# Six units' query softmax as ten per-row exponentials on ScalarE, and another queue for one of the last stores

## Chip, cores and metric

One core of one Trainium2 chip. The metric is device microseconds (us) of one execution. TensorE multiplies matrices, VectorE and GpSimd do elementwise work, ScalarE evaluates functions such as the exponential, and SyncE issues DMAs; ScalarE can issue DMAs too.

## What is computed

A linear attention feeds two gated MLPs. Cut to what matters:

```python
def _attn_ref(q, k, v):                       # 8 batches, 8 heads, 576 tokens, 64 columns
    q_s = q - np.max(q, axis=-1, keepdims=True)
    q_s = np.exp(q_s)
    q_s = q_s / (np.sum(q_s, axis=-1, keepdims=True) + 1e-09)
    k_s = softmax of k over the tokens        # axis=2, written out in the same way
    kv = np.einsum('bhsd,bhse->bhde', k_s, v)
    return np.einsum('bhsd,bhde->bhse', q_s, kv)

# x: 4608 tokens x 512
xn = x / rms(x) * rms_g
x = (silu(xn @ w_gate) * (xn @ w_val)) @ w_out        # d_ff 1536
h = x @ w_in
return (h * sigmoid(1.702 * h)) @ w_out2              # d_ff 2048
```

The query's softmax runs over 64 columns, so each token and head is a row of its own, with its own maximum and its own sum.

## The kernel before

**Units.** Attention is cut into 32 units: one batch and two heads each. In a unit the 576 tokens lie on 128 partitions, as R = 5 rows of each head on a partition, so a tile of queries is 128 partitions x 2 heads x 5 rows x 64 columns: 640 elements on a partition, in ten rows of 64. `unit_steps` gives nine steps for each unit. The steps that matter here:

- `s0`: VectorE reduces the keys to a maximum per column (line 337).
- `s1`: TensorE transposes that maximum (344), VectorE reduces it over the partitions (348), and VectorE takes the queries' maximum of each row, `qm` (351). Then the queries minus `qm` are written in place (352). `side` is GpSimd for units 0 to 7 and VectorE after them.
- `s2`: TensorE spreads the keys' maximum (356), VectorE subtracts it (357).
- `s3`: ScalarE takes the exponential of the keys, `ke`, and of the queries, `qe`, one instruction of 640 elements each (375). VectorE sums each query row into `qs` (381), adds 1e-9 (382) and takes the reciprocal (383); `side` multiplies `qe` by it (384).
- `s4` multiplies keys and values on TensorE (390) and scales the product on VectorE (398 to 407); the last four steps transpose the queries (420) and multiply them by it (441 to 445).

**Order.** All instructions are issued in the order in which the program is written; each engine works its own list in order, and a semaphore holds an instruction back until its inputs are there. Units 0 to 3 run first, interleaved by a sorted table, with little else beside them. Then the first MLP starts. It runs over nine token tiles `j`, and in each tile over slots of matmuls (556 for the gate, the value and, from the second tile on, the output; 586 for the output in the first tile). Units 4 to 7 lie among the slots of `j` = 0. In the same slots the weights are decoded for the first time: ScalarE (152, 153), VectorE (156, 157) and GpSimd (162) turn a fetched piece `stage` into fp32, and ScalarE and GpSimd split it into a high and a low half (165, 166). A matmul of three passes uses the high half in the first two and the low half in the third. The fetch of the next piece is issued after GpSimd's 162.

**End.** The last step of the second MLP writes its output `y` in four parts (p = 5, 3, 4, 2), each of two halves of 128 tokens: SyncE's queue takes the first half, ScalarE's the second (784). A half that crosses a border between token rows takes two stores.

Of the kernel before, what the change touches and what calls it, by code (L numbers as in the profile page):

```python
# [8 lines left out]
F32 = mybir.dt.float32  # L9
# [3 lines left out]
AF = mybir.ActivationFunctionType  # L13
ALU = mybir.AluOpType
AX = mybir.AxisListType
# [5 lines left out]
def attention_glu_mlp(  # L21
# [26 lines left out]
    nc = tc.nc  # L48
    B, H, S, D = q.shape
# [3 lines left out]
    P = 128  # L53

    R = S // P + 1
    FULL = (R - 1) * P
    REST = S - FULL
    NC = DM // P
# [25 lines left out]
    def f(x):  # L84
        return x.bitcast(F32)
# [4 lines left out]
    ap = tc.alloc_tile_pool(name="ap", bufs=1, side="right")  # L90
# [183 lines left out]
    kt, qt, vt = {}, {}, {}  # L274
# [23 lines left out]
    def load_kq(u):  # L298
        b, c = units[u]
        hs = slice(2 * c, 2 * c + 2)  # L300
        if u < NC:

            kt[u], qt[u] = (
                wp.tile([P, 2, R, D], F32, tag="w", bufs=NW, name=f"{n}_raw") for n in "kq"
            )
            pad(kt[u], qt[u])
        else:
            kt[u], qt[u] = k_sb, q_sb
        spread_tokens(kt[u], k[b, hs])
        spread_tokens(qt[u], q[b, hs])  # L310

    def load_v(u):
        b, c = units[u]
        if 2 <= u < NC:
            vt[u] = wp.tile([P, 2, R, VW], F32, tag="w", bufs=NW, name="v_raw")
            pad_v(vt[u])
        else:
            vt[u] = v_sb[u % 2]
        spread_tokens(vt[u], v[b, 2 * c : 2 * c + 2])

    def bank(tag):
        bufs = {"att": 2, "gv": 2, "acc": 4}[tag]
        return ps.tile([P, 512], F32, tag=tag, bufs=bufs, name=f"ps_{tag}")

    def unit_steps(u, tag="att"):
        b, c = units[u]
        st = {}
        kH, kL = kvH[u % 2], kvL[u % 2]

        side = nc.gpsimd if u < 2 * NC else nc.vector  # L330
        whole = u < NC
        if whole:
            kH = kvF[:, u % 2]

        def s0():
            m1 = ap.tile([P, 2, D], F32, tag="m1", bufs=2, name="m1")
            nc.vector.tensor_reduce(
                out=m1, in_=kt[u].rearrange("p h r d -> p h d r"), op=ALU.max, axis=AX.X
            )
            st["m1"] = m1  # L340

        def s1():
            t = bank(tag)
            nc.tensor.transpose(
                t[:, 0:P], st["m1"].rearrange("p h d -> p (h d)"), ident
            )
            m = ap.tile([P, 1], F32, tag="m", bufs=2, name="m")
            nc.vector.reduce_max(out=m, in_=t[:, 0:P], axis=AX.X)
            st["m"] = m
            qm = ap.tile([P, 2, R, 1], F32, tag="qm", bufs=2, name="qm")  # L350
            nc.vector.tensor_reduce(out=qm, in_=qt[u], op=ALU.max, axis=AX.X)
            side.tensor_tensor(qt[u], qt[u], qm.to_broadcast([P, 2, R, D]), op=ALU.subtract)

        def s2():
            t = bank(tag)
            nc.tensor.transpose(t[:, 0:P], st["m"].to_broadcast([P, P]), ident)
            nc.vector.tensor_tensor(
                kt[u],
                kt[u],
                t[:, 0:P]  # L360
                .rearrange("p (h o d) -> p h o d", h=2, o=1)
                .to_broadcast([P, 2, R, D]),
                op=ALU.subtract,
            )

        def s3():
            for n, src in (("k", kt.pop(u)), ("q", qt.pop(u))):
                st[n] = (wp if u < NC else ap).tile(
                    [P, R, 2, D],
                    F32,  # L370
                    tag="w" if u < NC else f"{n}e",
                    bufs=NW if u < NC else 1,
                    name=f"{n}e",
                )
                nc.scalar.activation(st[n].rearrange("p r h d -> p h r d"), src, AF.Exp)  # L375
            if NC <= u + 1 < len(units):
                load_kq(u + 1)
                load_v(u + 1)
            qe = st["q"]
            qs = ap.tile([P, R, 2, 1], F32, tag="qs", bufs=2, name="qs")  # L380
            nc.vector.tensor_reduce(out=qs, in_=qe, op=ALU.add, axis=AX.X)  # L381
            nc.vector.tensor_scalar_add(qs, qs, EPS_SUM)
            nc.vector.reciprocal(out=qs, in_=qs)
            side.tensor_tensor(qe, qe, qs.to_broadcast([P, R, 2, D]), op=ALU.mult)

        def s4():
            t = bank(tag)
            for r in range(R):
                for h in range(2):
                    nc.tensor.matmul(  # L390
                        t[h * D : (h + 1) * D, 0:VW],
                        st["k"][:, r, h],
                        vt[u][:, h, r, :],
                        start=(r == 0),
                        stop=(r == R - 1),
                    )
            rs = ap.tile([P, 1], F32, tag="rs", bufs=2, name="rs")
            nc.vector.tensor_scalar_add(rs, t[:, D : D + 1], EPS_SUM)
            nc.vector.reciprocal(out=rs, in_=rs)
            for h in range(2):  # L400
                a = slice(h * D, (h + 1) * D)
                nc.vector.tensor_scalar_mul(kH[a, a], t[a, 0:D], rs[a])
            if whole:
                return
            for h in range(2):
                a = slice(h * D, (h + 1) * D)
                nc.vector.scalar_tensor_tensor(
                    out=kL[a, a],
                    in0=t[a, 0:D],
                    scalar=rs[a],  # L410
                    in1=f(kH[a, a]),
                    op0=ALU.mult,
                    op1=ALU.subtract,
                )

        def qT(i):
            t = bank(tag)
            width = 0
            for r in halves_of(b)[i]:
                nc.tensor.transpose(  # L420
                    t[:, width : width + P],
                    st["q"][:, r].rearrange("p h d -> p (h d)"),
                    ident,
                )
                width += size(r)
            if whole:
                qF = ap.tile([P, HALF * P + REST], F32, tag="qH", bufs=2, name="qF")[:, :width]
                nc.scalar.activation(qF, t[:, :width], AF.Copy)
                st["q", i] = qF, None, width
                return  # L430
            hi = ap.tile([P, HALF * P + REST], F32R, tag="qH", bufs=2, name="qH")[:, :width]
            lo = ap.tile([P, HALF * P + REST], F32R, tag="qL", bufs=2, name="qL")[:, :width]
            nc.scalar.activation(hi, t[:, :width], AF.Copy)
            nc.vector.tensor_tensor(lo, t[:, :width], f(hi), op=ALU.subtract)
            st["q", i] = hi, lo, width

        def att(i):
            hi, lo, width = st["q", i]
            t = bank(tag)
            if whole:  # L440
                nc.tensor.matmul(t[:, :width], kH, hi, start=True, stop=True)
            else:
                nc.tensor.matmul(t[:, :width], kH, hi, start=True, stop=False)  # L443
                nc.tensor.matmul(t[:, :width], kH, lo, start=False, stop=False)  # L444
                nc.tensor.matmul(t[:, :width], kL, hi, start=False, stop=True)  # L445
            g0 = b * S + (sum(map(size, halves_of(b)[0])) if i else 0)
            done = 0
            while done < width:
                j, o = divmod(g0 + done, T)
                n = min(width - done, T - o)  # L450
                nc.scalar.activation(xraw(j, c)[:, o : o + n], t[:, done : done + n], AF.Copy)
                done += n

        return [
            s0, s1, s2, s3, s4,
            lambda: qT(0), lambda: qT(1), lambda: att(0), lambda: att(1),
        ]
# [404 lines left out]
    with tc.manual_schedule():  # L862
# [94 lines left out]
        for j in range(NTILE):  # L957
# [18 lines left out]
            for slot in range(SLOTS):  # L976
                n, part = divmod(slot, 3)
# [71 lines left out]
        for i in range(-1, END):  # L1049
            if i >= 0:  # L1050
                for c in range(2):
# [4 lines left out]
                        i, t, lambda i=i, c=c: sums(xraw2[i + 1, c], "B", (nc.vector,) * 4)  # L1056
# [64 lines left out]
        for k in range(NT // T * NSET):  # L1121
# [14 lines left out]
            u = ufac.pop(k)  # L1136
# [8 lines left out]
            for p in (6, 7, 5, 3, 1, 4, 2) if k in IN_PIECES else MADE:  # L1145
# [36 lines left out]
                if end and p in (5, 3, 4, 2):  # L1182
                    h, y = (0, y2) if p in (5, 4) else (1, y1)
                    part = slice(0, Q) if p in (5, 3) else slice(Q, DM)
                    for i, queue in enumerate((nc.sync, nc.scalar)):
                        store_out(first_token(g, i, h)[2], y[:, i, :], queue, part)
            if last and not end:
                for h, y in ((0, y2), (1, y1)):
# [49 lines left out]
```

## Time and profile before

| | |
|---|---|
| median of three runs | 1738.14 us (1737.97 to 1739.06) |
| the profiled execution, timed | 1738.99 us |
| its span in the profile | 1737.2 us |
| TensorE busy | 1711.2 us (99%) |
| VectorE busy | 1164.2 us (67%) |
| ScalarE busy | 778.8 us (45%) |
| GpSimd busy | 377.3 us (22%) |
| TensorE clock granted, mean | 0.999 of full speed |

The span runs from the first to the last recorded instruction or transfer; 1.79 us of the timed execution lie around it. Busy shares are means over stages that have different limits, so the stage around the change is what has to be read.

### The profile page before, as it was taken

The page shows a single profiled execution, that of the slowest core. Times are in us where ns is not written, and L with a number is a line of the kernel's source. Part 1 is how long each engine was busy: PE and PEld are TensorE (multiplying, and loading weights), DVE is VectorE, ACT ScalarE, POOL GpSimd, SP SyncE. Part 2 cuts the span into 40 slices and gives each one's busy share as a digit, 9 for nine tenths or more (in the row PEclk, how much of TensorE's full clock was granted, in tenths as well). Part 3 has the DMA queues.
Part 4 walks back from the last instruction along what each step waited for, and adds up shares of the span by engine and source line. Part 5 has one row for each costly group of instructions (what it writes and reads, how often), then busy time and mean ns, then how long its engine had stood idle before and what let it go on. Part 6 is the DMA issues. An engine that isn't in the chain of part 4 may idle for free.

```text
span 1737.2 us, 26461 instructions
## 1 busy us (share of the span) xinstructions
PE 1711.2 (99%) x10002; PEld 1509.9 (87%) x10002; DVE 1164.2 (67%) x1943; ACT 778.8 (45%) x1299; POOL 377.3 (22%) x352
## 2 busy tenths in 40 slices
PE   6999999999999999999999999999999999999998
PEld 4666888888888888888888899999999999999998
DVE  7998668667676676765234367556556887777786
ACT  5775544535455444534222345445445533333332
POOL 5775222222222212211112523110002500000000
PEclk9999999999999999999999999999999999999999
DMA  6564322313322233110001134554444664444432
GB/s 175 170 191 134 103 84 82 97 56 102 96 82 84 69 102 96 58 48 0 25 1 49 52 119 158 176 169 153 146 146 151 226 196 133 134 126 130 134 122 86
DMA packets 207632, 193.64 MB, mean 111 GB/s; under 512 B 58896, under 2 KB 188944, under 8 KB 207504
## 3 DMA queue, kind: packets, MB, share of 16 engines
q1 hardware_dynamic: 197376, 174.11, 32.6%
q10 hardware_dynamic: 10128, 17.83, 2.8%
q8 instruction: 79, 1.29, 0.3%
q14 instruction: 49, 0.40, 0.1%
HBM read 123.21 MB, written 68.68 MB: 110 GB/s over the span
## 4 chain that ended last, share of the span: by engine, by line
PE 89%; DVE 6%; ACT 2%; DMA 1%; issue 1%; POOL 0%; SPq 0%; DVEq 0%; ACTq 0%; POOLq 0%
PE ps_gv L556 29%; PE ps_out L1150 20%; PE ps_in L738 20%; PE ps_acc L556 14%; DVE xr L533 1%; PE ps_acc L586 1%; PE ps_att L390 1%; DVE sqa L521 1%; PE ps_att L420 1%; DVE w L157 1%; DVE w L156 0%; DMA stage<-in_moe_w_gate_dram 0%; PE ps_att L443 0%; PE ps_att L445 0%; PE ps_att L444 0%
## 5 line engine op out<-in xcount | busy, mean ns | idle before, releaser
L738 PE MATMUL ps_in<-xf,w2i 128*128 128x384 f32 x2016 | 350.3, 335 | 0.0
L738 PEld LDWEIGHTS ps_in<-xf,w2i 128*128 128x128 f32 x2016 | 349.9, 188 | 0.3 <-ACT h L750 0.2
L556 PE MATMUL ps_gv<-xs,wg 128*128 128x512 f32 x1296 | 320.4, 395 | 1.3 <-POOL xs L548 0.7
L556 PE MATMUL ps_gv<-xs,wv 128*128 128x512 f32 x1296 | 317.9, 394 | 1.6 <-POOL wv L166 1.5
L556 PEld LDWEIGHTS ps_gv<-xs,wg 128*128 128x128 f32 x1296 | 240.7, 188 | 58.8 <-DVE xs L548 2.9
L556 PEld LDWEIGHTS ps_gv<-xs,wv 128*128 128x128 f32 x1296 | 239.5, 188 | 52.0 <-POOL wv L166 3.0
L556 PE MATMUL ps_acc<-u,wo 128*128 128x512 f32 x1152 | 283.5, 395 | 0.0
L1150 PE MATMUL ps_out<-w2o,uf 128*128 128x256 f32 x2268 | 271.6, 282 | 0.0
L1150 PEld LDWEIGHTS ps_out<-w2o,uf 128*128 128x128 f32 x2268 | 269.6, 189 | 1.2 <-DVE uf L827 0.2
L556 PEld LDWEIGHTS ps_acc<-u,wo 128*128 128x128 f32 x1152 | 212.1, 188 | 44.2
L981 ACT ACTIVATE s<-ps_gv 128x512 f32<-128x512 f32 x108 | 64.6, 598 | 379.0 <-PE ps_gv L556 378.8
L166 POOL TENSOR_TENSOR wo<-raw,wo 128x512 fp32r<-128x512 f32 x96 | 126.7, 1320 | 490.4 <-ACT wo L165 381.1
L987 DVE TENSOR_TENSOR s<-s,ps_gv 128x512 f32<-128x512 f32 x108 | 73.5, 680 | 177.5 <-PE ps_gv L556 167.3
L723 ACT ACTIVATE h<-h 128x384 f32<-128x384 f32 x144 | 74.2, 525 | 111.6 <-DVE h L762 88.4
L162 POOL TENSOR_TENSOR w<-w,stage 128x512 int32<-128x512 int32 x56 | 76.4, 1364 | 195.6 <-PE ps_gv L556 61.9
L630 DVE TENSOR_TENSOR raw<-raw 128x256 f32<-128x256 f32 (+1 forms) x236 | 106.1, 492 | 9.4 <-DMA raw<-w2d 7.3
L762 DVE TENSOR_TENSOR h<-h,ps_in 128x384 f32<-128x384 f32 x144 | 77.8, 553 | 48.2 <-PE ps_in L738 48.1
L823 ACT ACTIVATE uf<-raw 128x1792 fp32r<-128x1792 f32 (+2 forms) x38 | 61.6, 1623 | 83.1 <-DVE raw L630 42.8
L1150 PE MATMUL ps_out<-w2oq,uf 128*128 128x256 f32 x756 | 90.9, 281 | 0.0
L381 DVE TENSOR_REDUCE qs<-qe 128x10 f32<-128x640 f32 x32 | 26.2, 820 | 95.7 <-ACT qe L375 95.6
L1150 PEld LDWEIGHTS ps_out<-w2oq,uf 128*128 128x128 f32 x756 | 90.1, 189 | 0.0
L827 DVE TENSOR_TENSOR uf<-raw,uf 128x1792 fp32r<-128x1792 f32 (+2 forms) x38 | 73.0, 1924 | 18.2 <-ACT uf L823 18.2
(153 smaller groups left out, 1965.4 us busy)
## 6 DMA issues: line engine op xcount, KB each, us to landing
u<-h SPq DMA_DIRECT2D x192, 192.0 KB, 1.9
stage<-in_moe_w_out_dram SPq DMA_DIRECT2D x28, 512.0 KB, 3.6
raw<-u SPq DMA_DIRECT2D x24, 512.0 KB, 4.4
x<-ev ACTq DMA_DIRECT2D x34, 256.0 KB, 2.0
stage<-in_moe_w_in_dram SPq DMA_DIRECT2D x16, 512.0 KB, 3.7
w2d<-w SPq DMA_DIRECT2D x32, 256.0 KB, 2.7
v_sb<-in_v_dram SPq DMA_DIRECT2D x60, 128.0 KB, 3.1
out_dram<-y ACTq DMA_DIRECT2D x29, 256.0 KB, 4.2
```

The costliest lines, as they stand in the source:

```text
L162: return scaled, signed, lambda: nc.gpsimd.tensor_tensor(dst, dst, lo, op=ALU.add)
L166: nc.gpsimd.tensor_tensor(dst[:, 1, :], src, f(dst[:, 0, :]), op=ALU.subtract)
L556: nc.tensor.matmul(t, w(a), x(e), start=first and i == 0, stop=last and i == 2)
L630: engine.tensor_tensor(raw[:, o], raw[:, a], raw[:, b], op=op)
L723: nc.scalar.activation(dst, src, AF.Gelu_apprx_sigmoid)
L738: nc.tensor.matmul(t, w[:, a, s, c * P : (c + 1) * P], xfac[i, p, c][:, e, :], start=p in (1, 6, 5) and c == 0 and k == 0, stop=c == 1 and ...
L762: nc.vector.tensor_tensor(v, v, t, op=ALU.add)
L823: nc.scalar.activation(ufac[k][:, 0, piece], uraw[k][:, 1:8][:, piece], AF.Copy)
L827: nc.vector.tensor_tensor(w[:, 1, piece], raw[:, piece], f(w[:, 0, piece]), op=ALU.subtract)
L981: nc.scalar.activation(s, tg, AF.Silu)
L987: nc.vector.tensor_tensor(s, s, tv, op=ALU.mult)
L1150: nc.tensor.matmul(t[:, i * Q : (i + 1) * Q], u[:, a, LEFT[p] - 1, i * P : (i + 1) * P], w[:, e, m % 2, :], start=m == 0 and i == 0 and n ...
```

## The change

Units 0, 1 and 4 to 7 (`rows`) take their queries' softmax in another way. VectorE negates `qm`, and nothing subtracts it from the queries. ScalarE runs ten exponentials of 64 elements in place of one of 640; each takes its row's negated maximum as a bias from memory and leaves the row's sum in `qs`. VectorE no longer sums these rows. Units 2, 3 and 8 to 31 stay as they were. At the end, the first half of the last part (p = 2) is stored through ScalarE's queue, like the second half.

```diff
+        rows = u < 2 or NC <= u < 2 * NC
...
             nc.vector.tensor_reduce(out=qm, in_=qt[u], op=ALU.max, axis=AX.X)
-            side.tensor_tensor(qt[u], qt[u], qm.to_broadcast([P, 2, R, D]), op=ALU.subtract)
+            if rows:
+                st["qm"] = qm
+                nc.vector.tensor_scalar_mul(qm, qm, -1.0)
+            else:
+                side.tensor_tensor(qt[u], qt[u], qm.to_broadcast([P, 2, R, D]), op=ALU.subtract)
...
-                nc.scalar.activation(st[n].rearrange("p r h d -> p h r d"), src, AF.Exp)
+                if n == "k" or not rows:
+                    nc.scalar.activation(st[n].rearrange("p r h d -> p h r d"), src, AF.Exp)
+                    continue
+                qs = ap.tile([P, R, 2, 1], F32, tag="qs", bufs=2, name="qs")
+                for r in range(R):
+                    for h in range(2):
+                        nc.scalar.activation(
+                            st[n][:, r, h],
+                            src[:, h, r],
+                            AF.Exp,
+                            bias=st["qm"][:, h, r],
+                            accum_out=qs[:, r, h],
+                        )
...
-            qs = ap.tile([P, R, 2, 1], F32, tag="qs", bufs=2, name="qs")
-            nc.vector.tensor_reduce(out=qs, in_=qe, op=ALU.add, axis=AX.X)
+            if not rows:
+                qs = ap.tile([P, R, 2, 1], F32, tag="qs", bufs=2, name="qs")
+                nc.vector.tensor_reduce(out=qs, in_=qe, op=ALU.add, axis=AX.X)
...
-                    for i, queue in enumerate((nc.sync, nc.scalar)):
+                    for i, queue in enumerate((nc.scalar if p == 2 else nc.sync, nc.scalar)):
```

In the rows of order below, line numbers of the change are higher by up to 18 than those of before for the same statement (381 of before is 399 of the change, 382 is 400, 383 is 401, 384 is 402).

On ScalarE, at the start of the program, before and then with the change (`k_raw` and `q_raw` are the loaded keys and queries of units 0 to 3, `qF` a transposed part of unit 0's queries):

```order
L375 ACTIVATE ke<-k_raw 128x2x5x64
L375 ACTIVATE qe<-q_raw 128x2x5x64
L375 ACTIVATE ke<-k_raw 128x2x5x64
L375 ACTIVATE qe<-q_raw 128x2x5x64
L428 ACTIVATE qF<-ps_acc 128x256
```

```order
L381 ACTIVATE ke<-k_raw 128x2x5x64
L386 ACTIVATE qe,qs<-q_raw,qm 128x64 x10
L381 ACTIVATE ke<-k_raw 128x2x5x64
L386 ACTIVATE qe,qs<-q_raw,qm 128x64 x10
L446 ACTIVATE qF<-ps_acc 128x256
```

Nothing changes place; one instruction of each of the two units becomes ten, and these ten also write `qs`.

On VectorE, for the same two units, before and then with the change (`m` is the keys' maximum; the row 348 or 349 in the middle opens unit 1, and the last row opens unit 2):

```order
L351 TENSOR_REDUCE qm<-q_raw 128x10
L357 TENSOR_TENSOR k_raw<-k_raw,ps_acc 128x640
L337 TENSOR_REDUCE m_298<-k_raw 128x128
L381 TENSOR_REDUCE qs<-qe 128x10
L382 TENSOR_SCALAR qs<-qs 128x10
L383 RECIPROCAL qs<-qs 128x10
L348 TENSOR_REDUCE m<-ps_acc 128x1
```

```order
L352 TENSOR_REDUCE qm<-q_raw 128x10
L355 TENSOR_SCALAR qm<-qm 128x10
L362 TENSOR_TENSOR k_raw<-k_raw,ps_acc 128x640
L338 TENSOR_REDUCE m_298<-k_raw 128x128
L400 TENSOR_SCALAR qs<-qs 128x10
L401 RECIPROCAL qs<-qs 128x10
L349 TENSOR_REDUCE m<-ps_acc 128x1
```

The sum of 381 is gone, a small multiplication stands ahead of the keys' subtraction, and the addition of 1e-9 now reads what ScalarE wrote; the next unit's `m` still stands behind it.

On GpSimd, in the slots of unit 5, before and then with the change (`wv`, `wg` and `raw` are weights, `q_sb` the queries):

```order
L162 TENSOR_TENSOR raw_816<-raw_816,stage 128x512
L352 TENSOR_TENSOR q_sb<-q_sb,qm 128x640
L166 TENSOR_TENSOR wv_860<-w_785,wv_860 128x512
L162 TENSOR_TENSOR w_855<-w_855,stage 128x512
L162 TENSOR_TENSOR w_873<-w_873,stage 128x512
L384 TENSOR_TENSOR qe<-qe,qs 128x640
L166 TENSOR_TENSOR wg_921<-w_855,wg_921 128x512
```

```order
L166 TENSOR_TENSOR wv_884<-w_809,wv_884 128x512
L162 TENSOR_TENSOR w_879<-w_879,stage 128x512
L162 TENSOR_TENSOR w_897<-w_897,stage 128x512
L402 TENSOR_TENSOR qe<-qe,qs 128x640
L166 TENSOR_TENSOR wg_953<-w_879,wg_953 128x512
```

The subtraction is gone; the low half of the next gate weight still stands behind the queries' product with the reciprocal.

## Rows read from the trace of the kernel before

**Rows 1.** The page: TensorE's busy time, its share of the span, and instructions.

```profile
PE 1711.2 (99%) x10002; PEld 1509.9 (87%) x10002; DVE 1164.2 (67%) x1943; ACT 778.8 (45%) x1299; POOL 377.3 (22%) x352
```

**Rows 2.** Windows: stretch, length, busy us (instructions) of PE, PEld, DVE, ACT, POOL.

```profile
0.00:30.00 30.00, 16.38 (x119) 11.28 (x120) 22.70 (x53) 14.94 (x30) 15.66 (x34) 1.00 0.82 216
...
60.00:80.00 20.00, 19.57 (x95) 13.30 (x95) 18.68 (x25) 15.06 (x26) 15.22 (x12) 1.00 0.62 181
...
140.00:180.00 40.00, 39.98 (x173) 27.60 (x171) 28.20 (x35) 23.30 (x39) 17.41 (x13) 1.00 0.40 123
```

**Rows 3.** Timeline of VectorE, units 0 and 1: start us, duration us, instruction, [idle before].

```profile
9.84 0.82 DVE L381 TENSOR_REDUCE qs<-qe 128x10 f32<-128x640 f32 x1 [0.31 <-ACT qe L375]
10.70 0.17 DVE L382 TENSOR_SCALAR qs<-qs 128x10 f32<-128x10 f32 x1
...
11.04 0.23 DVE L348 TENSOR_REDUCE m<-ps_acc 128x1 f32<-128x128 f32 x1
...
14.82 0.82 DVE L381 TENSOR_REDUCE qs<-qe 128x10 f32<-128x640 f32 x1
15.67 0.17 DVE L382 TENSOR_SCALAR qs<-qs 128x10 f32<-128x10 f32 x1
...
16.13 0.29 DVE L348 TENSOR_REDUCE m<-ps_acc 128x1 f32<-128x128 f32 x1
```

**Rows 4.** Timeline of ScalarE, units 0 and 1.

```profile
8.45 0.74 ACT L375 ACTIVATE ke<-k_raw 128x640 f32<-128x640 f32 x1 [6.21 <-DMA v_sb<-in_v_dram]
9.09 0.72 ACT L375 ACTIVATE qe<-q_raw 128x640 f32<-128x640 f32 x1
12.76 0.74 ACT L375 ACTIVATE ke<-k_raw 128x640 f32<-128x640 f32 x1 [2.94 <-DVE k_raw L357]
```

**Rows 5.** Timeline of all engines around unit 5, 71 to 81 us.

```profile
71.02 1.37 POOL L352 TENSOR_TENSOR q_sb<-q_sb,qm 128x640 f32<-128x640 f32 x1 [0.57 <-DVE qm L351]
71.31 1.63 DVE L157 SCALAR_TENSOR_TENSOR w<-stage,w 128x512 int32<-128x512 int32 x1
...
76.26 0.72 ACT L375 ACTIVATE qe<-q_sb 128x640 f32<-128x640 f32 x1
...
77.02 0.82 DVE L381 TENSOR_REDUCE qs<-qe 128x10 f32<-128x640 f32 x1 [0.92 <-ACT qe L375]
...
77.73 3.70 PE L586 MATMUL ps_acc<-s,raw 128*128 128x512 f32 x8
77.87 0.17 DVE L382 TENSOR_SCALAR qs<-qs 128x10 f32<-128x10 f32 x1
...
79.68 1.73 POOL L166 TENSOR_TENSOR wg<-w,wg 128x512 fp32r<-128x512 f32 x1
```

**Rows 6.** ScalarE's groups by form: instructions, busy us, mean ns of one.

```profile
L981 ACT ACTIVATE s<-ps_gv 128x512 f32<-128x512 f32 x108 | 64.6, 598 | 379.0 <-PE ps_gv L556 378.8
...
L516 ACT ACTIVATE sqa<-ps_att,eps_sb 128x512 f32<-128x512 f32 x7 | 4.8, 687 | 0.1
...
L451 ACT ACTIVATE xr<-ps_acc 128x64 f32<-128x64 f32 x4 | 0.9, 222 | 0.0
...
L860 ACT ACTIVATE warm<-eps_sb 128x1 f32<-128x1 f32 x2 | 0.4, 203 | 0.0
```

**Rows 7.** Timeline of ScalarE, two instructions back to back.

```profile
27.16 0.20 ACT L860 ACTIVATE warm<-eps_sb 128x1 f32<-128x1 f32 x1
27.27 0.36 ACT L451 ACTIVATE xr<-ps_acc 128x256 f32<-128x256 f32 x1
```

**Rows 8.** Timeline from 42 us: one decode step, and a wait of TensorE.

```profile
44.30 0.69 DVE L157 SCALAR_TENSOR_TENSOR w<-stage,w 128x512 int32<-128x512 int32 x1
...
53.06 2.56 PE L556 MATMUL ps_gv<-xs,wv 128*128 128x512 f32 x10 [1.05 <-POOL wv L166]
```

**Rows 9.** The last stores' issues by queue: duration ns min/median/max, first and last start us.

```profile
L784 SPq DMA_DIRECT2D out_dram<-y x6: 426/545/592, 1730.8 to 1734.0; - x6
L784 ACTq DMA_DIRECT2D out_dram<-y x4: 338/362/377, 1730.8 to 1733.4; - x4
```

## The prediction

> **What bounds the kernel now.** I read the page first: TensorE is busy for 1711.2 of 1737.2 us [rows 1], so a change elsewhere counts only where TensorE waits. Windows of the first part, where the six units lie, show where that is [rows 2]. In the first 30 us TensorE works for 16.38 us and VectorE for 22.70. From 60 to 80 us TensorE is at 19.57 of 20 us, but VectorE is at 18.68 and ScalarE and GpSimd at 15: the engines are nearly balanced, and what a helper loses soon becomes a wait of TensorE. From 140 us on TensorE is full (39.98 of 40) and nothing is to be gained or lost there. So two places count: units 0 and 1, and units 4 to 7.
>
> At the first place the timeline of VectorE tells the order of events [rows 3]. VectorE sums unit 0's queries at 9.84, when ScalarE has just given them (it waited 0.31 us for that), adds 1e-9 at 10.70 and opens unit 1 at 11.04 (line 348). The same steps of unit 1 are at 14.82, 15.67 and 16.13, where unit 2 opens. All that follows stands behind this list: each microsecond by which line 348 of unit 2 moves, the first MLP's start moves too, since units 2 and 3 then run on as before.
>
> At the second place, unit 5 for instance, the exponential of the queries starts at 76.26, VectorE waits 0.92 us for it, sums at 77.02 and adds 1e-9 at 77.87 [rows 5]. GpSimd needs the reciprocal for its product (384) and makes the gate weight's low half (166) behind that: from 79.68 to 81.41. TensorE's matmuls before that gate weight end at 81.43 (77.73 + 3.70), and it wants the low half two matmuls later. The low half is there only a few tenths early. So ScalarE's exponential stands at the head of a chain through VectorE and GpSimd to TensorE that has almost no slack.
>
> **The price of one row.** The change puts ten exponentials of 64 elements where one of 640 stood, and everything hangs on how often ScalarE can start one; call that x us. No row shows one with a row's sum. An instruction of 128x64 lasts 0.222 us and one of 128x1 0.203 [rows 6]; of the latter, 0.11 us after its start at 27.16 the next one starts [rows 7], so 0.09 of it overlaps, and a 128x64 without a bias from memory comes every 0.13 us. A bias from memory: 0.687 us with it (516) against 0.598 without (981), both 128x512 from PSUM, so 0.09 more [rows 6]. That makes 0.22. The sum must be written besides. Below, that is free, x = 0.22, and if the bias hides in the overlap too, x = 0.13. If the write costs as much as the smallest instruction of ScalarE with its overlap, 0.11, x = 0.33. If nothing overlaps, 0.22 + 0.09 + 0.20 gives x = 0.51. I take 0.33: ten sums of ten rows are ten writes more, and the nearest row for a write is the smallest instruction.
>
> On this the page "ScalarE: Activation LUTs" of the Trainium skill (What ACT_TABLE_LOAD costs) speaks against the change: it counts 186 ns + 0.833 ns an element, 93 ns more for a bias from memory, and lets 93 ns overlap. Its estimate for 64 elements is thus x = 0.24; it gives no price for the sum. The rows agree with its parts (0.222 for 128x64, 0.09 for the bias). With its 0.24 the sum below would be +3.5 us, 1741.6.
>
> **Units 0 and 1.** The keys' exponential and then the queries' start 0.64 us apart (8.45, 9.09) [rows 4]. The new multiplication is of the form of line 382, 0.17 us [rows 3], and delays the start by as much. The addition of 1e-9 then runs at 9.09 + 0.17 + 10x instead of 10.70: later by 10x - 1.4. VectorE has nothing else to do meanwhile, as the next row in its list, line 348 of unit 1, stands behind. In unit 1 the keys' exponential starts 1.72 us after line 348 (11.04, 12.76), the queries' 0.64 + 0.17 after that, so the addition runs 2.53 + 10x behind line 348, before 4.63 (11.04, 15.67): later by another 10x - 2.1, and never better than -0.68, since VectorE's own work ahead of it fills 3.78 us (11.04 to 14.82) and 0.17. With x = 0.33 that is 1.9 + 1.2 = **+3.1 us**. The two sums saved on VectorE (0.86 each, 9.84 to 10.70) are in it. GpSimd's subtraction (1.37 us in unit 5 [rows 5]) no longer stands between VectorE and the exponential, but it lay beside the keys' exponential and gives nothing more.
>
> **Units 4 to 7.** From the start of the queries' exponential to the addition there are 1.61 us (76.26, 77.87) [rows 5]; after, 10x. The other three repeat unit 5 within 0.03 us. With x = 0.33 the product, the gate weight's low half and all behind them come 1.7 us later, of which I let a slack of 0.2 swallow a part (bounds 0 and 0.5, the two matmuls): 1.5 a unit, **+6.0 us** for four. Unit 4's subtraction also kept GpSimd from a value weight, for which TensorE waited 1.05 us [rows 8]; that wait goes, but TensorE then stands at the gate weight that much earlier and waits for the same low half, so I cost it at nothing. The ten rows also hold up ScalarE's decoding behind them, by 10x - 0.63 = 2.7 us; it had been done in time for a VectorE that now itself comes 1.7 later, so at most a few tenths come on top, left in the range.
>
> **The last stores.** SyncE's queue starts its last issue at 1734.0, ScalarE's at 1733.4, with 0.36 us an issue against 0.55 [rows 9]. With the first half moved, ScalarE issues at 1733.4 and 1733.8: **-0.2 us**.
>
> **The sum.** 3.1 + 6.0 - 0.2 = +8.9 us. The profiled execution, 1738.99, would become 1747.9; it lies 0.85 above the median of the runs, so I forecast a median of 1747.0. As a function of x the sum is 60x - 10.9 (20x from the first two units, 40x from the others), with break-even at x = 0.18.
>
> **Rivals.**
>
> *The rows start as fast as rows without bias and sum (not slower).* At x = 0.13 units 0 and 1 give -0.8 (-0.1 and the floor of -0.68), units 4 to 7 at most 0.3 each, the stores 0.2: -2.2 us, 1735.9. For it speaks that ten rows in one list wait for nothing; against it the 0.09 us of the bias [rows 6]. It decides below x = 0.18. Chance 0.14.
>
> *The sum is free, the bias is not.* x = 0.22 gives +2.3 us, 1740.4, inside what a measurement of this kernel can tell from no change, which is about 0.2% or 3.5 us. Chance 0.14.
>
> *Nothing overlaps.* x = 0.51 gives +19.7 us, 1757.8, if each sum has to be fetched before the next exponential starts. Against it is that ScalarE's neighbours overlap everywhere in the timeline. Chance 0.12.
>
> *GpSimd's rest helps VectorE.* Line 157 takes 0.69 us alone [rows 8] and 1.63 beside GpSimd's subtraction [rows 5]. With the subtraction gone VectorE could get 0.94 back in each of units 4 to 7: -3.8, leaving +5.1 us, 1743.2. Against it: the next of GpSimd's instructions moves up into the place, and VectorE waits for ScalarE afterwards in any case (0.92 in unit 5). The page "GPSIMD Engine Reference" of the Trainium skill (Specifications) says that GpSimd shares its SBUF interfaces with VectorE, which the two durations bear out. Chance 0.08. If it came on top of the first rival, that one would give -6.0 us.
>
> **How the numbers follow.** The forecast, x from 0.28 to 0.45 (+6 to +16 us), has 0.52. Slower by over 0.2%: forecast, no overlap and GpSimd's rest, 0.72. Within 0.2%: the free sum, 0.14, and 0.06 of the first rival, 0.20. Faster by over 0.2%: what is left of the first rival, together with GpSimd's rest and waits that I don't see, 0.08. The range goes from 1737.5 (x = 0.17) to 1757.0 (x = 0.50); it leaves out the first rival and the top of "nothing overlaps".
>
> **What would show it.** In the changed kernel's timeline: x as the distance of two rows of 128x64; line 348's successor for unit 2 near 19.2 us instead of 16.13; VectorE waiting for ScalarE ahead of the addition by about 2 us in units 4 to 7; TensorE's window from 60 to 80 us at 18 instead of 19.57 busy; the last store's issue from ScalarE at the end. The prediction is wrong if x lies below 0.25, or if TensorE in units 4 to 7 doesn't wait for the gate weight although the low half comes late, which would mean more slack than I read from the ends of modelled matmuls.

## The result, and the profile after

| | before | after |
|---|---|---|
| median | 1738.33 us (1737.97 to 1739.06, 4 runs) | 1750.34 us (1749.79 to 1750.91, 4 runs) |
| profiled execution, timed | 1738.99 us | 1749.79 us |
| its span | 1737.2 us | 1748.0 us |

The ratio is 1.0069, with an interval from 1.0051 to 1.0086: the changed kernel is slower by 12.0 us. Forecast were 8.9 more, from 1737.5 to 1757.0. The granted clock was 0.999 in both profiled executions.

The page of the changed kernel answers to [rows 1] (busy us, share of the span, instructions):

```profile
PE 1711.2 (98%) x10002; PEld 1507.2 (86%) x10002; DVE 1157.9 (66%) x1943; ACT 794.0 (45%) x1413; POOL 368.7 (21%) x346
```

TensorE's work is the same to a tenth of a microsecond. VectorE and GpSimd have less to do than before, ScalarE 15 us more, and ScalarE is busy for only 45% of the span. Nothing on this page says why the kernel is slower; the stages do. The windows of the first part of the changed kernel, to be read against [rows 2] (stretch, length, busy us of PE, PEld, DVE, ACT, POOL, granted clock, DMA share, GB/s):

```profile
0.00:30.00 30.00, 13.44 (x91) 9.11 (x91) 20.49 (x48) 17.36 (x59) 10.83 (x30) 1.00 0.78 201
60.00:80.00 20.00, 17.30 (x68) 11.37 (x67) 18.48 (x29) 14.38 (x26) 13.83 (x11) 1.00 0.58 177
...
140.00:180.00 40.00, 40.00 (x157) 27.72 (x156) 32.71 (x35) 22.56 (x39) 23.34 (x17) 1.00 0.44 132
```

TensorE lost 2.94 us of work in the first 30 us (16.38, 13.44), and 2.27 us between 60 and 80 us (19.57, 17.30). From 140 us on it is as full as before. All that was lost was lost by then, and it was not given back.

**A row and its sum.** The timeline of ScalarE in the changed kernel, unit 0, then the start of unit 1; it answers to [rows 4]:

```profile
7.77 0.74 ACT L381 ACTIVATE ke<-k_raw 128x640 f32<-128x640 f32 x1 [5.54 <-DVE k_raw L362]
8.41 0.33 ACT L386 ACTIVATE qe<-q_raw,qm 128x64 f32<-128x64 f32 x1
8.65 0.19 ACT L386 ACTIVATION_READ_ACCUMULATOR qe<-q_raw,qm 128x1 f32 x1
8.74 0.33 ACT L386 ACTIVATE qe<-q_raw,qm 128x64 f32<-128x64 f32 x1
...
14.52 0.74 ACT L381 ACTIVATE ke<-k_raw 128x640 f32<-128x640 f32 x1 [2.71 <-POOL qe L402]
```

Each row is two instructions: the exponential, and a second one of a single element that writes the sum. Two rows start 0.33 us apart (8.41, 8.74). Unit 5's ten rows below take 3.31 us (80.56 to 83.87), so x is 0.331. It was forecast as 0.33.

**Units 0 and 1.** The timeline of VectorE in the changed kernel, which answers to [rows 3] (line 349 is 348 of before, 400 is 382):

```profile
5.74 0.29 DVE L349 TENSOR_REDUCE m<-ps_acc 128x1 f32<-128x128 f32 x1 [0.63 <-PE ps_acc L345]
...
6.79 0.17 DVE L355 TENSOR_SCALAR qm<-qm 128x10 f32<-128x10 f32 x1
...
11.85 0.17 DVE L400 TENSOR_SCALAR qs<-qs 128x10 f32<-128x10 f32 x1 [3.00 <-ACT qe L386]
...
12.19 0.23 DVE L349 TENSOR_REDUCE m<-ps_acc 128x1 f32<-128x128 f32 x1
...
13.18 0.54 DVE L355 TENSOR_SCALAR qm<-qm 128x10 f32<-128x10 f32 x1
...
18.60 0.17 DVE L400 TENSOR_SCALAR qs<-qs 128x10 f32<-128x10 f32 x1 [2.12 <-ACT qe L386]
...
19.06 0.29 DVE L349 TENSOR_REDUCE m<-ps_acc 128x1 f32<-128x128 f32 x1
```

The same timeline of the kernel before has unit 0's row of line 348 here:

```profile
6.62 0.29 DVE L348 TENSOR_REDUCE m<-ps_acc 128x1 f32<-128x128 f32 x1 [0.63 <-PE ps_acc L344]
```

Two traces are compared by distances, since their first loads land at different times (this row is 0.88 us earlier after). From line 348 of unit 0 to that of unit 1 it was 4.42 us (6.62, 11.04) and is 6.45: 2.03 more. From there to unit 2 it was 5.09 (11.04, 16.13) and is 6.87: 1.78 more. Together 3.81. (Line 349 of unit 2 was forecast near 19.2 and starts at 19.06, but that is luck: without the 0.88 us it would have been 19.94.) VectorE does nothing during these waits of 3.00 and 2.12 us: the addition of 1e-9 needs the last of the ten sums, and the next unit's maximum stands behind it in VectorE's list.

**Units 4 to 7.** The timeline of all engines around unit 5 of the changed kernel, which answers to [rows 5]:

```profile
76.37 0.69 DVE L157 SCALAR_TENSOR_TENSOR w<-stage,w 128x512 int32<-128x512 int32 x1
...
80.56 0.33 ACT L386 ACTIVATE qe<-q_sb,qm 128x64 f32<-128x64 f32 x1
...
81.84 3.70 PE L604 MATMUL ps_acc<-s,raw 128*128 128x512 f32 x8
...
83.87 0.65 ACT L152 ACTIVATE raw<-stage 128x512 f32<-128x512 f32 x1
84.00 0.17 DVE L400 TENSOR_SCALAR qs<-qs 128x10 f32<-128x10 f32 x1 [4.53 <-ACT qe L386]
...
84.59 1.50 POOL L402 TENSOR_TENSOR qe<-qe,qs 128x640 f32<-128x640 f32 x1 [3.59 <-ACT raw L152]
84.99 0.61 ACT L165 ACTIVATE wg<-w 128x512 fp32r<-128x512 f32 x1
...
85.66 0.73 PE L574 MATMUL ps_gv<-xs,wg 128*128 128x512 f32 x2
86.06 1.72 POOL L166 TENSOR_TENSOR wg<-w,wg 128x512 fp32r<-128x512 f32 x1
...
87.83 2.37 PE L574 MATMUL ps_gv<-xs,wg 128*128 128x512 f32 x9 [1.44 <-POOL wg L166]
```

TensorE does two matmuls with the gate weight's high half and then waits 1.44 us for its low half. The waits of TensorE from 44 to 150 us in the changed kernel (total us, times, longest) begin with this line:

```profile
PE ps_gv L574 <- POOL wg L166: 5.8, 4, 1.5
```

Four waits, one for each of units 4 to 7. In the kernel before the list of the same stretch names none for the gate weight. The product, the high half and TensorE's matmuls stand as follows in the kernel before, unit 5:

```profile
78.03 0.61 ACT L165 ACTIVATE wg<-w 128x512 fp32r<-128x512 f32 x1
...
78.47 1.26 POOL L384 TENSOR_TENSOR qe<-qe,qs 128x640 f32<-128x640 f32 x1 [0.82 <-DVE qs L383]
...
80.87 3.34 PE L556 MATMUL ps_gv<-xs,wg 128*128 128x512 f32 x12
```

So the way from the start of the queries' exponential to the end of the low half can be laid side by side. Before: 76.26 to 81.41, 5.15 us. After: 80.56 to 87.78, 7.22 us. The addition starts 1.61 after the exponential before and 3.44 after the change (+1.83); from there to the product it is 0.60 and 0.59; the product takes 1.26 and 1.50 (+0.24); the low half 1.73 and 1.72. That is 2.07 us more for this unit.

The list of waits leaves out a part. The ends of matmuls are modelled: by them the eight ahead of the gate weight end at 85.54 (81.84 + 3.70), and almost nothing is idle before the start at 85.66. Starts show the wait: before, the first matmul with the gate weight starts 3.14 us after the eight ahead of it (77.73 [rows 5], 80.87); after, it starts 3.82 us after them (81.84, 85.66), 0.06 us behind the end of ScalarE's high half (84.99 + 0.61 = 85.60). So TensorE waits for both halves in turn: 0.68 us longer for the high half, then 1.44 for the low one, together the 2.1 us of this unit. In units 4, 6 and 7 the first wait is 1.1, 0.7 and 0.7 us, by the same distances. The four units together lose 3.2 us there and 5.8 at the low half. The waits for a value weight, 1.5 us before, are gone, and those for `qL` ahead of line 345 (344 of before) grow from 0.7 to 1.7.

**The end.** The last stores' issues in the changed kernel, by queue, answer to [rows 9] (duration ns min, median, max; first and last start us; the x40 holds earlier parts as well):

```profile
L802 ACTq DMA_DIRECT2D out_dram<-y x40: 333/458/1134, 1427.1 to 1744.6; - x40
...
L802 SPq DMA_DIRECT2D out_dram<-y x5: 426/546/589, 1741.7 to 1744.2; - x5
```

The last issue starts 3.4 us before the span's end (1744.6 of 1748.0), where it was 3.2 (1734.0 of 1737.2). The queue that ends last is now ScalarE's; the end did not come closer.

### The profile page after: what moved, and what is told of

Read it like the earlier page. It is cut to its first block, busy times and chain, and to the rows that moved or that the text cites. A ratio compares the mean times of both kernels' runs of the same rounds, so it can differ in the third digit from the quotient of the medians.

```text
span 1748.0 us, 26561 instructions
## 1 busy us (share of the span) xinstructions
PE 1711.2 (98%) x10002; PEld 1507.2 (86%) x10002; DVE 1157.9 (66%) x1943; ACT 794.0 (45%) x1413; POOL 368.7 (21%) x346
## 4 chain that ended last, share of the span: by engine, by line
PE 88%; DVE 6%; ACT 3%; issue 1%; SPq 1%; POOL 1%; DMA 0%; DVEq 0%; ACTq 0%; POOLq 0%
PE ps_gv L574 29%; PE ps_out L1168 20%; PE ps_in L756 20%; PE ps_acc L574 13%; DVE xr L551 1%; PE ps_att L408 1%; DVE sqa L539 1%; PE ps_acc L604 1%; PE ps_att L438 1%; ACT qe L386 1%; DVE w L156 0%; PE ps_att L461 0%; DVE s L1005 0%; PE ps_att L463 0%; PE ps_att L462 0%
## 5 line engine op out<-in xcount | busy, mean ns | idle before, releaser
L399 DVE TENSOR_REDUCE qs<-qe 128x10 f32<-128x640 f32 x26 | 21.3, 820 | 92.7 <-ACT qe L381 92.7
```

## The experiments

All were timed in five rounds against the kernel before, whose median was 1737.98 us beside the first four, 1738.25 beside the next four and 1738.13 beside the last two (21 runs each). Gains and losses below are against the one beside them.

**The parts alone.** The first three kernels take the change apart: the rows in units 0 and 1, the rows in units 4 to 7, and the stores.

```diff
-        rows = u < 2 or NC <= u < 2 * NC
+        rows = u < 2                       # e1, and the stores as before
+        rows = NC <= u < 2 * NC            # e2, and the stores as before
```

The third is the kernel before with the new stores:

```diff
-                    for i, queue in enumerate((nc.sync, nc.scalar)):
+                    for i, queue in enumerate((nc.scalar if p == 2 else nc.sync, nc.scalar)):
```

Units 0 and 1:

> Ten row exponentials in units 0 and 1 alone; units 4 to 7 and the stores as before. The prediction's term for these two units, 20x - 3.5 with the x = 0.33 us that the changed kernel's timeline shows, gives +3.1 us, about 1741.4. Rival: VectorE's list has slack later on that takes the delay back; then under +1 us.

Units 4 to 7:

> Ten row exponentials in units 4 to 7 alone. The prediction's term is +6.0 us (1744.3); the changed kernel's trace, in which TensorE falls back by 8.0 us between its first gate matmul and the end of unit 7's slots, says +8.0 (1746.3). Rival: the two places are not independent, and these units alone cost all of the +12, or less than 5.

Stores:

> Only the last part's first half stored through ScalarE's queue. The prediction says -0.2 us; the changed kernel's profile, whose last VectorE step lies 4.38 us before the end against 4.43 before, says -0.05. Both are below what five rounds can tell; more than 1 us either way would be against both.

| | median | against before | ratio, interval |
|---|---|---|---|
| e1, units 0 and 1 | 1741.91 us | +3.9 us | 1.0024 (1.0015 to 1.0032) |
| e2, units 4 to 7 | 1746.05 us | +8.1 us | 1.0048 (1.0035 to 1.0060) |
| e3, stores | 1738.04 us | +0.1 us | 1.0001 (0.9992 to 1.0010) |

The three add to 12.1 us, the change to 12.0: within these intervals the parts don't touch each other. Line 348 in e1, VectorE's timeline, units 0, 1 and 2:

```profile
6.53 0.29 DVE L349 TENSOR_REDUCE m<-ps_acc 128x1 f32<-128x128 f32 x1 [0.63 <-PE ps_acc L345]
...
12.98 0.23 DVE L349 TENSOR_REDUCE m<-ps_acc 128x1 f32<-128x128 f32 x1
...
19.85 0.29 DVE L349 TENSOR_REDUCE m<-ps_acc 128x1 f32<-128x128 f32 x1
```

The distances are 6.45 and 6.87, as in the whole change, and the 3.81 us that they are longer than before are near the 3.9 that the kernel lost. In units 4 to 7 e2 loses 2.0 us a unit, nearly all of the 2.07 by which the way through unit 5 got longer: there was no slack to speak of.

**The price of the bias and of the sum.** Two kernels keep ten exponentials in the six units, each with one half of the new form (stores as before). In the first GpSimd subtracts the maximum as before and the rows keep their sums; in the second the rows take the bias and VectorE sums as before.

```diff
-            if rows:
-                st["qm"] = qm
-                nc.vector.tensor_scalar_mul(qm, qm, -1.0)
-            else:
+            if True:
                 side.tensor_tensor(qt[u], qt[u], qm.to_broadcast([P, 2, R, D]), op=ALU.subtract)
...
-                            bias=st["qm"][:, h, r],
```

> Six units with ten row exponentials that keep the row's sum but have no bias from memory; GpSimd subtracts the maximum as before. Stores as before. Theory that bias and sum each add about 0.09 to 0.10 us to a row: x = 0.23 to 0.24, units 0 and 1 +1.3 us, units 4 to 7 0.7 to 1.2 each, together +4 to +6, 1742.4 to 1744.4. Rival, the sum forces each row to finish before the next: x stays at 0.33 or more and the time near 1750.

```diff
-                            accum_out=qs[:, r, h],
...
-            if not rows:
-                qs = ap.tile([P, R, 2, 1], F32, tag="qs", bufs=2, name="qs")
-                nc.vector.tensor_reduce(out=qs, in_=qe, op=ALU.add, axis=AX.X)
+            qs = ap.tile([P, R, 2, 1], F32, tag="qs", bufs=2, name="qs")
+            nc.vector.tensor_reduce(out=qs, in_=qe, op=ALU.add, axis=AX.X)
```

> Six units with ten row exponentials with the negated maximum as bias, but no sum on ScalarE: VectorE sums the rows as before. Stores as before. Theory: x = 0.24, and with VectorE's sum of 0.86 us behind it the addition comes 1.9 and 1.3 us later in units 0 and 1 and 1.7 to 2.1 in each of units 4 to 7: +10 to +12 us, 1748 to 1750, so the sum on ScalarE (0.09 a row, 0.9 a unit) only replaces what VectorE gave up. Rival: VectorE's sum was the dear part and ten rows alone cost little; then near 1742 or less if x were small, or clearly above 1752 if the sum on ScalarE had been nearly free.

With the sum and no bias: 1743.40 us, +5.4, ratio 1.0035 (1.0022 to 1.0047). With the bias and no sum: 1748.51 us, +10.3, ratio 1.0059 (1.0046 to 1.0071). ScalarE's timeline of the first, in unit 0:

```profile
8.96 0.24 ACT L383 ACTIVATE qe<-q_raw 128x64 f32<-128x64 f32 x1
9.10 0.19 ACT L383 ACTIVATION_READ_ACCUMULATOR qe<-q_raw 128x1 f32 x1
9.19 0.24 ACT L383 ACTIVATE qe<-q_raw 128x64 f32<-128x64 f32 x1
```

and of the second, with its ten rows in one line:

```profile
8.79 2.48 ACT L385 ACTIVATE qe<-q_raw,qm 128x64 f32<-128x64 f32 x10
```

The first has a row every 0.24 us (8.96, 9.19 and so on, ten from 8.96 to 11.10). In the second, ten rows of 0.33 end after 2.48 us, so they start (2.48 - 0.33) / 9 = 0.239 us apart. In the change it is 0.331. So the bias costs 0.09 us a row, and the sum 0.09 as well.

At the same x of 0.24 the kernel with VectorE's sum loses 4.9 us more than the one without. That is near six times the 0.86 us of the sum (9.84 to 10.70 [rows 3]), as it would be if the sum stood on the way that ends last, whichever engine makes it. The two also differ in how the maximum is taken off (GpSimd's subtraction against VectorE's multiplication), so the 4.9 are not the sum's alone. The change, which moves it to ScalarE for 10 x 0.09 = 0.9 us a unit, gains nothing by that; at +12.0 it is even 1.7 us behind the kernel with VectorE's sum, though the two intervals overlap. The traces give a reason: with VectorE's sum the high half of unit 5 is there at 85.21 (84.60 + 0.61) for matmuls that start at 85.51, 3.14 us after the eight ahead of them as in the kernel before, and units 5 to 7 lose only 1.51 us each at the low half. And the bias, another 0.9 us a unit, takes from GpSimd a subtraction that, as a later experiment shows, cost nothing in the kernel before. The change pays for both with time on the one engine that others wait for.

**Which of the two ways to the low half holds TensorE.** GpSimd's low half stands behind its product with the reciprocal, and it needs what ScalarE decodes behind the ten rows. The next kernel is the changed one with the product one step later in units 4 to 7, behind the gate weight's low half; another has the same in the kernel before.

```diff
-            side.tensor_tensor(qe, qe, qs.to_broadcast([P, R, 2, D]), op=ALU.mult)
+            st["mul"] = lambda: side.tensor_tensor(
+                qe, qe, qs.to_broadcast([P, R, 2, D]), op=ALU.mult
+            )
+            if not NC <= u < 2 * NC:
+                st["mul"]()
...
+            if NC <= u < 2 * NC:           # start of s4
+                st["mul"]()
```

> The changed kernel with the queries' product by the reciprocal (units 4 to 7) issued one step later on GpSimd, behind the gate weight's low half. Theory that TensorE waits for that low half only because it stands behind the product: the wait of 1.44 us at the gate weight falls to about 0.8 (ScalarE's high half is late too), part of it comes back at the value weight, 1 to 2.6 us gained in all, 1747.7 to 1749.3. Rival, that the decoding behind the ten rows on ScalarE holds TensorE: no change within 0.5 us.

> The kernel before with the same late product. Theory that the low half is there just in time before the change: no wait to remove, 0 to -0.8 us, the same within the measurement. Rival, that a wait is hidden in the modelled matmuls ahead of the gate weight (0.3 us or more a unit): -1.2 us or better.

The first gave 1750.46 us, ratio 1.0068 (1.0055 to 1.0081), against 1.0069 for the change: nothing was gained. The second gave 1738.74, ratio 1.0003 (0.9994 to 1.0012), the same as before. The theory that the low half waits only because it stands behind the product has fallen. Unit 5 in the first, TensorE and GpSimd:

```profile
85.95 0.73 PE L580 MATMUL ps_gv<-xs,wg 128*128 128x512 f32 x2
85.98 1.28 POOL L166 TENSOR_TENSOR wg<-w,wg 128x512 fp32r<-128x512 f32 x1 [4.63 <-ACT wg L165]
...
87.31 2.56 PE L580 MATMUL ps_gv<-xs,wg 128*128 128x512 f32 x10 [0.63 <-POOL wg L166]
88.49 1.45 POOL L402 TENSOR_TENSOR qe<-qe,qs 128x640 f32<-128x640 f32 x1
89.91 1.73 POOL L166 TENSOR_TENSOR wv<-w,wv 128x512 fp32r<-128x512 f32 x1
...
91.69 1.66 PE L580 MATMUL ps_gv<-xs,wv 128*128 128x512 f32 x6 [0.68 <-POOL wv L166]
```

The low half now waits for ScalarE's high half (165), which comes late by itself. TensorE's first matmul with the gate weight comes as late as in the change (3.84 us after the start of the eight ahead of it, at 82.11), and it still waits 0.63 us for the low half; the product has moved in front of the next weight's low half, for which TensorE waits 0.68. The wait was split, not removed.

**VectorE's and GpSimd's own work.** The kernel before, with neither the queries' maximum nor its subtraction in units 0 to 7 (this part of the computation is left out):

```diff
+            if u < 2 * NC:
+                return
             nc.vector.tensor_reduce(out=qm, in_=qt[u], op=ALU.max, axis=AX.X)
             side.tensor_tensor(qt[u], qt[u], qm.to_broadcast([P, 2, R, D]), op=ALU.subtract)
```

> The kernel before, with whole exponentials, in which units 0 to 7 leave out the queries' maximum and its subtraction (the softmax is the same without it up to rounding). This takes 0.63 to 0.81 us of VectorE and one GpSimd instruction from each unit and adds nothing to ScalarE. Theory, ScalarE heads the chain: units 0 to 3 gain only about 0.1 us each, because TensorE's transposed maximum comes no earlier, units 4 to 7 gain the 1.05 and 0.41 us that TensorE waited for the value weight behind the subtraction: -1 to -2 us. Rival, VectorE's and GpSimd's work is what bounds these stages: -4 us or better.

1738.14 us, ratio 0.9998 (0.9990 to 1.0007): the same, and a miss of the one or two microseconds expected. The queries' maximum on VectorE and the subtraction on GpSimd (1.37 us in unit 5 [rows 5]) were covered in all eight units; TensorE's waits for a value weight are gone, but those for `qL` ahead of the transpose of the keys' maximum (344) are longer (0.7 to 1.7 us). In the kernel before, what the change takes from these two engines was thus worth nothing.

**The ten rows behind the decoding.** The last two kernels change the order in units 4 to 7: in a slot the keys' exponential comes first, then the weights' decoding and splitting, then the queries' exponential, and its addition, reciprocal and product one step later. The next unit's loads, which follow the queries' exponential in the program, move behind it too. One has the ten rows (and stores as before), the other is the kernel before with its whole exponentials.

```diff
+        def s3_late():
...
+            nc.scalar.activation(
+                st["k"].rearrange("p r h d -> p h r d"), kt.pop(u), AF.Exp
+            )
...
+            behind.append(queries)         # the queries' exponential(s), and the next loads
+            st["weigh"] = weigh            # addition, reciprocal, product: end of s4
...
-            s0, s1, s2, s3, s4,
+            s0, s1, s2, s3_late if NC <= u < 2 * NC else s3, s4,
...
+                    for fn in behind:
+                        fn()
+                    behind.clear()
```

> Rows only in units 4 to 7, stores as before; in the slots of these units the weights' decoding and splitting is now written ahead of the ten exponentials of the queries, and the addition of 1e-9, the reciprocal and GpSimd's product come one step later. Theory (the loss comes from what stands behind the ten rows on ScalarE and, through VectorE's wait for the last sum, on VectorE and GpSimd): at least 5 of the 8 us that the rows in units 4 to 7 alone cost come back, 1739 to 1741; up to 0.7 us a unit may stay, since a later value weight's high half can come late. Rival (ten rows cost ScalarE 2.6 us more a unit, and TensorE loses it wherever they stand): within 1.5 us of the 1746 of the rows in units 4 to 7 alone.

> The kernel before, its whole exponentials kept, with the same new order in units 4 to 7 (decoding and splitting first, then the queries' exponential, sum, reciprocal and product one step later). It tells whether the order alone is worth anything. Theory: the whole exponential holds up the decoding by 0.7 us only, and TensorE's waits of that stage are about 1 us in all, so the same as before within 1 us. Rival (the order itself gains): 1736 or below.

With the ten rows: 1741.54 us, +3.4, ratio 1.0018 (1.0009 to 1.0026). With the whole exponentials: 1741.62 us, +3.5, ratio 1.0020 (1.0011 to 1.0029). In this order the kernel with ten rows takes as long as the one with whole exponentials, within these intervals; in the order of before the rows cost 8.1 us more. Unit 5 with the rows, ScalarE, GpSimd, TensorE and VectorE:

```profile
77.77 0.62 ACT L165 ACTIVATE wg<-w 128x512 fp32r<-128x512 f32 x1
...
78.29 0.33 ACT L421 ACTIVATE qe<-q_sb,qm 128x64 f32<-128x64 f32 x1
...
78.47 1.28 POOL L166 TENSOR_TENSOR wg<-w,wg 128x512 fp32r<-128x512 f32 x1 [1.37 <-ACT wg L165]
...
81.05 3.34 PE L613 MATMUL ps_gv<-xs,wg 128*128 128x512 f32 x12
...
81.73 0.17 DVE L434 TENSOR_SCALAR qs<-qs 128x10 f32<-128x10 f32 x1 [1.13 <-ACT qe L421]
...
82.33 1.26 POOL L436 TENSOR_TENSOR qe<-qe,qs 128x640 f32<-128x640 f32 x1 [1.34 <-DVE qs L435]
...
83.55 0.62 ACT L165 ACTIVATE wv<-w 128x512 fp32r<-128x512 f32 x1
...
84.25 1.49 POOL L166 TENSOR_TENSOR wv<-w,wv 128x512 fp32r<-128x512 f32 x1 [0.66 <-ACT wv L165]
...
85.79 2.57 PE L613 MATMUL ps_gv<-xs,wv 128*128 128x512 f32 x10 [0.61 <-POOL wv L166]
```

Both halves of the gate weight are there before TensorE comes to it, and all twelve matmuls run without a wait. Two things moved here, the decoding and the product; the kernel with the late product shows that the product alone gains nothing, and the decoding alone was not tried. The rival, by which ten rows cost their 2.6 us of ScalarE wherever they stand, has fallen. My theory held in kind but not in all of its size: 4.7 us of the 8.1 came back where at least 5 were expected, and for the whole exponentials I expected no change. The order itself, with the late loads, costs 3.5 us. TensorE's waits from 44 to 150 us in the kernel with the rows begin with the value weight:

```profile
PE ps_gv L613 <- POOL wv L166: 2.3, 4, 0.7
```

That is 2.3 us in four waits, 1.5 in two before. In unit 5 the product is done at 83.59, but GpSimd then idles 0.66 us until ScalarE has the value weight's high half, which is now decoded behind the ten rows (units 6 and 7 show the same, 0.67 and 0.68 us; in unit 4 the product stands directly in front of the low half). This is the "up to 0.7 us a unit" that the theory left open. So the rows are not free in this order; they hold up a later weight.

The kernel with whole exponentials loses much of its 3.5 us elsewhere. VectorE's maximum of the next unit's keys waits for their load:

```profile
87.05 1.34 DVE L339 TENSOR_REDUCE m<-k_sb 128x128 f32<-128x640 f32 x1 [2.02 <-DMA k_sb<-in_k_dram]
```

It waits 1.97 us for the load in another unit; before, the same row (337) waits for no load. `qL` stands behind it on VectorE, and TensorE's waits for `qL` are 2.9 us where they were 0.7. So the like losses of the two kernels don't have one cause. The rest I have not traced to single waits, and how much of it the late loads cost was not tested.

## Why the prediction was right, and where its sizes were off

**What bounds.** The two places were the right ones. TensorE lost its time in the first 30 us and in units 4 to 7, and nothing after 140 us. From 60 to 80 us it works for 17.30 us; forecast was 18.

**The price of a row.** x was taken as 0.33 and is 0.331. Its parts came out near what was built: 0.09 for the bias, as taken, and 0.09 for the sum where I took 0.11 from ScalarE's smallest instruction. That was a good proxy for a plain reason: the sum is written by such an instruction (0.19 us, where the smallest took 0.203 [rows 6]). For a row with neither this leaves 0.15 (no kernel ran one) where I took 0.13, so two misses of 0.02 cancel, and the agreement to 0.001 is luck. By the figures of the Trainium skill's page "ScalarE: Activation LUTs" (What ACT_TABLE_LOAD costs) the estimate for a row with bias and without its sum was 0.24; the kernel with just that measured 0.239. With 0.331 the rivals "as fast as plain rows", "the sum is free" and "nothing overlaps" have all fallen, and so has the whole side below the break-even of 0.18.

**Units 0 and 1: +3.1 forecast, +3.9 measured.** The mechanism was right. Unit 0 lost 2.03 us for 1.9. Unit 1 lost 1.78 for 1.2, because the new multiplication was costed from line 382, at 0.17 us. It takes that in unit 0 (6.79), but 0.54 in unit 1 (13.18 to 13.72), beside GpSimd's product for unit 0 (12.43 to 13.69). The other 0.13 or so in each unit is the time from the last row's end to the addition, which the formula "10x" left out: 83.87 to 84.00 in unit 5.

**Units 4 to 7: +6.0 forecast, +8.1 measured.** The step that failed is "of which I let a slack of 0.2 swallow a part", together with "at most a few tenths come on top". I laid one chain, through VectorE, GpSimd's product and the low half, at 1.7 us. It got longer by 2.07 in unit 5: 1.83 to the addition (10x and the 0.13), and 0.24 on the product (1.50 us in units 5 to 7, 1.26 in unit 4; why is open). The slack was not there. I had counted the two matmuls from 81.43, the modelled end of the matmuls ahead; but the matmuls with the gate weight start at 80.87, twelve in 3.34 us, so the third is due at about 81.4, just when the low half is done (81.41). And the second way, ScalarE's decoding behind the rows, was worked out rightly as 2.7 us later (the high half starts 1.77 us after the queries' exponential before, 4.43 after: +2.66), but not as something that could hold TensorE. It can: TensorE's first matmul with the gate weight starts 0.06 us after the high half is done, 0.68 us late. With the product out of the way TensorE waits for what comes behind the late high half instead, and the time stays; only in the kernel with the decoding ahead of the rows, and the product late, does the wait for the gate weight go. "It had been done in time for a VectorE that now itself comes 1.7 later" looked at one consumer, and forgot that TensorE and GpSimd's low half need ScalarE's high half directly. The multiplication, 0.77 us here (75.25 to 76.02), lies ahead of the exponential and costs nothing that shows.

**The last stores: -0.2 forecast, 0 measured.** In the profile the earlier issue did not bring the end closer: the last issue starts 3.4 us before the end and not 3.2. What ends after it I did not follow. The time is the same within an interval of 0.1%, or 1.7 us, which cannot tell -0.2 from nothing.

**GpSimd's rest helps VectorE.** The relief came: line 157 takes 0.69 us where it took 1.63. But it gained nothing, as the argument against it said. VectorE then waits for ScalarE for 4.53 us, and not about 2 as I wrote: 0.92 before, 1.83 by which the addition is later, 0.82 for the sum that it no longer makes and about 0.9 by which VectorE is through its earlier work sooner give 4.5. Line 157 runs twice in that stretch, and I had counted it once: it gains 0.94 and 1.00 us (1.63 and 1.69 before, 0.69 twice after), of which the multiplication and a slower line 156 take about 1.0 back. Here the work taken from VectorE became a longer wait.

Together the misses are 0.8 for the first units, 2.1 for the others and 0.2 for the stores: 3.1 us, which is how 8.9 became 12. That all of them go the same way, and still end within the range, owes something to the range's width of 19.5 us.

## What to carry to other kernels

Before one ScalarE instruction is cut into many, look at what stands behind it on ScalarE's list and who waits for the last piece, not at ScalarE's busy share: here 45% busy hid a loss of 12 us, and where the weights' decoding went first the same ten rows cost no more than one whole exponential, though that order itself cost 3.5 us. When two ways lead to the same waiting instruction, work out the delay on both; taking away the one that shows leaves the other. Compare the starts of TensorE's matmuls, too, not only the list of waits: in three of four units 0.7 us stood in no list here. Work taken off an engine gains nothing where that engine has to wait afterwards, as VectorE did here.

## What the runs showed that I had not expected

- The sum of a row is not part of the exponential: each is an instruction of its own on ScalarE, 0.187 us in the mean of 60, of which 0.09 is seen in the distance between rows.
- An exponential with a bias lasts longer in the trace (0.33 us against 0.24), and starts 0.09 us further from the next one.
- A VectorE instruction of 128x10 took 0.17 us in unit 0, 0.54 in unit 1 and 0.77 in unit 5, while line 400, of the same form, took 0.17 each time. The slow ones run beside GpSimd's product (12.43 to 13.69) and low half (74.68 to 75.98), and each ends 0.03 to 0.04 us after GpSimd's instruction does; in unit 0 GpSimd rests. The kernel before shows it as well: line 382 takes 0.81 us in unit 4, from 55.79 to 56.60, beside GpSimd's 162 (55.25 to 56.55). That GpSimd is the cause was not tested by itself.
